# Attention backward: a PSUM bank of their own for the narrow gradient sums, and a two-step pattern of who turns dS

## The chip, the cores and the metric

The kernel runs on one core of a Trainium2 chip. The metric is the device time of one execution in microseconds (us), the median of several. A profile comes from one execution more, recorded with the hardware profiler: its span runs from the first to the last instruction.

## What is computed

Four layers are run forward and then differentiated: linear attention (A), sliding-window attention (B), A, B, each with a layer norm ahead and a residual around. The tensors are bfloat16, with 2,048 tokens, width 640, 32 heads of 20. The change lies in the backward of the two B layers. Their forward is:

```
scores = einsum("bhqd,bhkd->bhqk", q, k) * (Dh ** -0.5)
mask   = (idx[:, None] - idx[None, :] >= 0) & (idx[:, None] - idx[None, :] < 256)
p      = softmax(where(mask, scores, -1e9))
o      = einsum("bhqk,bhkd->bhqd", p, v)
out    = x + o.reshape(B, S, D) @ wo
```

The outputs are the result and the gradients of the input and of the four weight matrices.

## The kernel before

The program is the forward (L311 on), the backward's first phase, `B_attn_bwd` for layer 3 (L1291), a phase of projections and layer A, `B_attn_bwd` for layer 1, and a last phase. Only `B_attn_bwd` and its table `ORDER` (L37) are touched by the diff.

`B_attn_bwd` goes over 8 groups of 4 heads. A group has 16 tiles of 128 tokens and 15 steps, one for each query tile (the first step takes tiles 0 and 1 together): 120 steps. With a window of 256, a query tile sees three key tiles, so a step has three 128x128 blocks for each of 4 heads. Each step is cut into two half-steps of two heads, numbered h = 2n + p for step n, p 0 or 1. A half-step consists of

- `mm_s` (L1331, on TensorE): scores of two heads, into a `pair` tile in PSUM (128 x 2 x 512 float32, 4,096 bytes of a partition; three of them take turns);
- `act_exp` (L1351, ScalarE): the exponential, read from the pair tile, written to `e_sb`; GpSimd masks two of the three blocks (L1355, L1358);
- `mm_dp` (L1331): dP of the same two heads, into the same pair tile, over the scores;
- `dve_ds` (L1366, VectorE): dS = dP * e * scale, read from the pair tile and `e_sb`, written to `ds_sb`;
- the turn of dS, since dQ needs dS with the other axis ahead. Either TensorE turns it (`pe_turn`, L1384: six 128x128 transposes into a PSUM tile `dsT_ps`, 1,536 bytes of a partition, two of them) and VectorE or ScalarE copies it to SBUF (`copy_t`, L1387, into `dsT`), or a DMA turns it straight from `ds_sb` to `dsT` (`dma_turn`, issued by SyncE at L305);
- the narrow products (`products`, L1399 and L1403, TensorE): dQ, dK and dV of one token tile, 20 columns wide (padded to 32), summed over up to three blocks. Two heads take 18 matmuls of 128x32.

Where the narrow sums go: columns 384 to 480 of each half of a pair tile are free. `pair_acc` (L1410) writes the sums of two heads there, into the pair tile of half-step h + 2, and `pair_evac` (L1420) copies them out of it to `dqkv` (120 elements of a partition), by ScalarE or VectorE as the table says. In one step of each group but the first, two token tiles are ready; then `quad_acc` (L1423) puts all four heads of one of them into a `dsT_ps` buffer, and ScalarE copies 240 elements out of it (L1427).

The order of the work is written out by hand. Each piece gets a time in half-steps (L1464 to 1479) and the pieces are emitted in order of these times; each engine runs its own pieces in that order, and waits by semaphore for others. dS of half-step h stands at h, `mm_s` of h + 3 at h + 0.1, `mm_dp` of h + 2 at h + 0.15, `act_exp` of h + 3 at h + 0.7. The rest comes from `ORDER[p][kind]`: when to turn, when and on which engine to copy, when to do the narrow sums, when and on which engine to copy these. The kind is 0 for a step whose two halves are both turned by TensorE, 1 for a step whose second half is turned by DMA, 2 for such a step before another of its kind. `by_dma` (L1370) decides: within a group, steps 0, 2, 4 and 6 are turned by TensorE alone and the other eleven have their second half turned by DMA, except in the last six steps of all.

Between two engines that read the same pair tile the program puts a wait too: `dve_ds` of a half-step waits for the copy that takes narrow sums out of its pair tile.

Of the kernel before, what the change touches and what calls it, by code (L numbers as in the profile page):

```python
# [32 lines left out]
def dve_ns(n):  # L33
# [1 line left out]


ORDER = (  # L37
    ((0.3, 1.05, "ACT", 0.6, 1.6, "DVE"), (1.3, 2.25, "DVE", 0.6, 1.6, "ACT"), (2.3, 3.5, "DVE", 0.6, 1.05, "ACT")),
    ((0.7, 2.25, "DVE", 0.6, 1.3, "ACT"), (0.3, 1.8, "ACT", 0.6, 1.3, "ACT"), (2.05, 1.8, "DVE", 0.25, 1.3, "ACT")),
)  # L40


# [137 lines left out]
class Kern:  # L180
# [1110 lines left out]
    def B_attn_bwd(self, l, dqkv, slab0=None, first=None):  # L1291
        nc, tc, D, T, TT, H, G, DP = self.nc, self.tc, self.D, self.T, self.TT, self.H, self.G, self.DP
        ld, E, DS, PR, TPS, TSB, ACC = {}, {}, {}, {}, {}, {}, {}
        with ExitStack() as st:
            def pool(name, **kw):
                return st.enter_context(tc.tile_pool(name=f"Bb{l}_{name}", bufs=1, reuse_waits="tile", **kw))
# [3 lines left out]
            slab1, pe, pps = pool("slabB"), pool("pe"), pool("ps", space=bass.MemoryType.PSUM)  # L1300
# [9 lines left out]
            NB = TT - 1  # L1310
            NS = G * NB
# [28 lines left out]
            def mm_dp(h):  # L1340
                if h < 2 * NS:
                    by_head(h, PR[h], "dOT", "VT")
# [25 lines left out]
                    in1=E[n][:, hs], op0=ALU.mult, op1=ALU.mult)  # L1368

            def by_dma(n):  # L1370
                return n % NB not in (0, 2, 4, 6) and n < NS - 6

            def dma_turn(h):
                n, p = divmod(h, 2)
# [3 lines left out]

            def pe_turn(h):
                n, p = divmod(h, 2)  # L1380
                ps = TPS[h] = pps.tile([P, 2, 3, P], BF, name="dsT_ps", bufs=2)
                for i in range(2):
                    for j in range(3):
                        nc.tensor.transpose(ps[:, i, j, :], DS[n][:, 2 * p + i, j, :], self.ident)  # L1384

            def copy(eng, out, in_):
                (nc.vector.tensor_copy if eng == "DVE" else nc.scalar.copy)(out, in_)  # L1387
# [5 lines left out]
            def products(g, t, hhs, out):  # L1393
                dq = [(k, *place(g, t, k)) for k in range(max(t - 2, 0), t + 1)]
                dkv = [(q, *place(g, q, t)) for q in range(t, min(t + 3, TT))]
                for hh in hhs:
                    cs = slice(HPAD * hh, HPAD * (hh + 1))
                    for i, (k, n, j) in enumerate(dq):
                        nc.tensor.matmul(out(hh, 0), lhsT=TSB[2 * n + hh // 2][:, hh % 2, j, :],  # L1399
                                         rhs=ld[g]["K"][:, k, cs], start=(i == 0), stop=(i == len(dq) - 1))  # L1400
                    for x, (src, rhs) in enumerate(((DS, "Q"), (E, "dO"))):
                        for i, (q, n, j) in enumerate(dkv):
                            nc.tensor.matmul(out(hh, 1 + x), lhsT=src[n][:, hh, j, :],  # L1403
                                             rhs=ld[g][rhs][:, q, cs], start=(i == 0), stop=(i == len(dkv) - 1))

            def spare(h):

                return PR[h][:, :, 3 * P:3 * P + 3 * HPAD].rearrange("p i (s c) -> p i s c", c=HPAD)

            def pair_acc(g, t, p, h):  # L1410
                if h not in PR:
                    PR[h] = pps.tile([P, 2, 512], F32, name=f"pair{h % 3}")
                products(g, t, (2 * p, 2 * p + 1), lambda hh, x: spare(h)[:, hh % 2, x, :])

            def grads(g, t, hh, nh):
                o = (4 * g + hh) * DH
                return dqkv[:, t, :].rearrange("p (s x) -> p s x", s=3)[:, :, o:o + nh * DH].rearrange(
                    "p s (h d) -> p h s d", d=DH)

            def pair_evac(g, t, p, h, eng):  # L1420
                copy(eng, grads(g, t, 2 * p, 2), spare(h)[:, :, :, 0:DH])

            def quad_acc(g, t):  # L1423
                ACC[g, t] = pps.tile([P, 4, 3, HPAD], F32, name="dsT_ps", bufs=2)
                products(g, t, range(4), lambda hh, x: ACC[g, t][:, hh, x, :])

            def quad_evac(g, t, eng):  # L1427
                copy(eng, grads(g, t, 0, 4), ACC.pop((g, t))[:, :, :, 0:DH])

            outs = {}  # L1430
            for g in range(G):
# [7 lines left out]
            with tc.manual_schedule(engines={mybir.EngineType.PE, mybir.EngineType.DVE, mybir.EngineType.SP,  # L1439
                                             mybir.EngineType.Activation, mybir.EngineType.Pool}):  # L1440
                for h in range(3):
                    mm_s(h)
                    act_exp(h)
                for h in range(2):
                    mm_dp(h)
                items, todo = [], []

                def at(when, f, *args):
                    items.append((when, len(items), f, args))

                def load(n):
                    if n % NB == 0:
                        todo[:] = loads(n // NB + 1) if n // NB + 1 < G else next_weights()
                    if todo:
                        todo.pop(0)()

                for h in range(2 * (NS + 4)):
                    n, p = divmod(h, 2)
                    kind = 0 if not by_dma(n) else 2 if by_dma(n + 1) else 1
                    turn, cp, cp_eng, acc, ev, ev_eng = ORDER[p][kind]  # L1460
                    if n < NS:
                        if not p and n % NB % 2 == 0:
# [93 lines left out]
```

## Time and profile before

| | |
|---|---|
| median of 3 runs | 2328.52 us (2324.72 to 2328.61) |
| the profiled execution | 2327.18 us |
| its span | 2325.2 us |
| mean granted TensorE clock | 0.945 of full |
| TensorE, matmuls | 2023.2 us busy, 87% of the span |
| TensorE, weight loads | 1405.2 us, 60% |
| VectorE | 1463.7 us, 63% |
| ScalarE | 1182.6 us, 51% |
| GpSimd | 852.3 us, 37% |

PE is TensorE, PEld its weight loads, DVE VectorE, ACT ScalarE, POOL GpSimd, SP SyncE (SPq its queue). A row of the timeline reads: start in the span, length, engine, line of the kernel, operation, output <- input, shape, count, and in brackets the idle time of the engine just before and what ended it. In a row of waits stand the waiter, what ended the wait, the us in total, the number of times and the longest. A row by stretches gives the ends, the length, the busy us of PE, PEld, DVE, ACT and POOL with their instruction counts, the granted TensorE clock, the busy share of the DMA engines and GB/s. In a row by lines stand busy us and mean ns of one, then the idle time before. Matmuls overlap in TensorE's pipeline, so a busy PE is not a PE at its peak, and the distance from start to start tells more than the length.

Costly groups of the two stages, over the whole span:

```profile
L1366 DVE SCALAR_TENSOR_TENSOR ds_sb<-pair,e_sb 128x768 bf16<-128x768 f32 x480 | 457.5, 954 | 79.9 <-ACT dqkv L1387 43.9
L1351 ACT ACTIVATE e_sb<-pair 128x768 bf16<-128x768 f32 x480 | 389.6, 813 | 144.8 <-PE pair L1331 134.3
L1384 PE MATMUL dsT_ps<-ident,ds_sb 128*128 128x128 bf16 x1896 | 171.3, 231 | 0.5 <-ACT dsT L1387 0.3
```

### The profile page before, as it was taken

How to read it: one execution, taken by the hardware profiler on the slowest of the kernel's cores; microseconds unless marked ns; L12 is line 12 of the kernel's file. 1: busy time of each engine (PE TensorE's matmuls, PEld its weight loads, DVE VectorE, ACT ScalarE, POOL GpSimd, SP SyncE). 2: the span in 40 equal slices, each digit the busy share in tenths (PEclk: the TensorE clock that was granted, in tenths of full speed). 3: DMA queues.
4: the chain of work that ended last, by engine and by line, in shares of the span. 5: the costliest groups of instructions: out<-in, count | busy, mean ns of one | idle time of the engine just before them, and what ended most of it. 6: DMA issues, size and time to landing. Idle time of an engine off the chain costs nothing. (4 is left out here: it accounts for less than half of the span.)

```text
span 2325.2 us, 67576 instructions
## 1 busy us (share of the span) xinstructions
PE 2023.2 (87%) x27798; PEld 1405.2 (60%) x27798; DVE 1463.7 (63%) x3048; ACT 1182.6 (51%) x2091; POOL 852.3 (37%) x1851
## 2 busy tenths in 40 slices
PE   6879899888887688888889979997888888998999
PEld 4556566555555456666656657754666665665674
DVE  6657677555564488898943328912998885443551
ACT  4527787527787137787832213311888783210330
POOL 1015455315666245555522203311555552221120
PEclk9989999879999798899999989998999899998999
DMA  7658999646675768898887789737898988987973
GB/s 256 198 140 192 209 203 216 169 125 161 151 157 126 197 165 150 136 155 147 155 192 171 160 191 196 181 85 157 147 151 148 148 147 171 193 187 177 214 171 100
DMA packets 968103, 389.22 MB, mean 167 GB/s; under 512 B 860401, under 2 KB 939889, under 8 KB 967537
## 3 DMA queue, kind: packets, MB, share of 16 engines
q1 hardware_dynamic: 931488, 351.24, 72.7%
q10 hardware_dynamic: 36304, 33.67, 4.5%
q8 instruction: 217, 3.56, 0.7%
q14 instruction: 94, 0.76, 0.1%
HBM read 115.34 MB, written 114.95 MB: 99 GB/s over the span
## 5 line engine op out<-in xcount | busy, mean ns | idle before, releaser
L1366 DVE SCALAR_TENSOR_TENSOR ds_sb<-pair,e_sb 128x768 bf16<-128x768 f32 x480 | 457.5, 954 | 79.9 <-ACT dqkv L1387 43.9
L1351 ACT ACTIVATE e_sb<-pair 128x768 bf16<-128x768 f32 x480 | 389.6, 813 | 144.8 <-PE pair L1331 134.3
L626 ACT ACTIVATE e_sb<-s_ps 128x1536 bf16<-128x1536 f32 (+2 forms) x256 | 350.8, 1370 | 91.9 <-PE s_ps L621 44.6
L630 POOL TENSOR_SCALAR_AFFINE_SELECT e_sb<-e_sb 128x256 bf16<-128x256 bf16 x512 | 216.9, 447 | 457.2 <-ACT e_sb L626 455.0
L849 PEld LDWEIGHTS <-om 128*128 128x128 bf16 x1920 | 191.3, 100 | 179.9 <-DMA om<-o 21.5
L849 PE MATMUL mm_ps<-wq,dqT 128*128 128x320 bf16 x1920 | 282.3, 302 | 10.4 <-DMA dqT<-dqkv 10.2
L1358 POOL TENSOR_SCALAR_AFFINE_SELECT e_sb<-e_sb 128x256 bf16<-128x256 bf16 x448 | 183.0, 408 | 259.0 <-ACT e_sb L1351 253.7
L849 PE MATMUL mm_ps<-dqkv,om 128*128 128x480 bf16 x1280 | 271.2, 370 | 0.0
L1015 POOL TENSOR_TENSOR gw<-w,gcar 128x640 f32<-128x640 f32 x64 | 89.6, 1399 | 457.2 <-ACT w L1012 442.9
L1331 PE MATMUL pair<-KTg,QTg 32*128 32x384 bf16 (+2 forms) x1024 | 169.6, 336 | 93.3 <-DVE ds_sb L1366 80.0
L1355 POOL TENSOR_SCALAR_AFFINE_SELECT e_sb<-e_sb 128x256 bf16<-128x256 bf16 x512 | 207.4, 408 | 86.1 <-ACT e_sb L1351 86.1
L849 PEld LDWEIGHTS <-dqT 128*128 128x128 bf16 x1920 | 186.1, 99 | 84.9 <-DMA dqT<-dqkv 11.0
L1399 PE MATMUL pair<-Ksl,dsT 128*128 128x32 bf16 x2712 | 217.7, 179 | 0.0
L1403 PE MATMUL pair<-Qsl,ds_sb 128*128 128x32 bf16 x2824 | 214.0, 177 | 0.0
L1403 PE MATMUL pair<-dOsl,e_sb 128*128 128x32 bf16 x2824 | 213.8, 177 | 0.0
L997 ACT ACTIVATE dh<-mm_ps 128x320 f32<-128x320 f32 x128 | 56.0, 438 | 304.4 <-PE mm_ps L849 238.1
L399 PE MATMUL mm_ps<-Wqkv_B,hnTB 128*128 128x320 bf16 x960 | 184.2, 308 | 5.4 <-DMA hnTB<-hnB 3.8
L655 PEld LDWEIGHTS <-e_sb 128*128 128x128 bf16 x2880 | 130.7, 97 | 81.2 <-DVE e_sb L635 18.5
L1399 PEld LDWEIGHTS <-dsT 128*128 128x128 bf16 x2880 | 153.2, 98 | 42.6 <-issue 42.6
L1331 PE MATMUL pair<-VTg,dOTg 32*128 32x384 bf16 (+2 forms) x1024 | 169.7, 337 | 10.0 <-DMA dOTg<-dOpt 7.0
L655 PE MATMUL pv_ps<-v_slab,e_sb 128*128 128x32 bf16 x2880 | 155.3, 178 | 22.0 <-POOL e_sb L638 6.6
L1384 PE MATMUL dsT_ps<-ident,ds_sb 128*128 128x128 bf16 x1896 | 171.3, 231 | 0.5 <-ACT dsT L1387 0.3
(154 smaller groups left out, 3705.3 us busy)
## 6 DMA issues: line engine op xcount, KB each, us to landing
qkvp<-qk_slab SPq DMA_DIRECT2D x32, 512.0 KB, 3.1
e<-ee SPq DMA_DIRECT2D x32, 320.0 KB, 2.5
kv<-kv SPq DMA_DIRECT2D x32, 320.0 KB, 2.7
o<-o SPq DMA_DIRECT2D x64, 160.0 KB, 3.2
om<-o SPq DMA_DIRECT2D x20, 512.0 KB, 4.7
hn<-hn SPq DMA_DIRECT2D x64, 160.0 KB, 2.9
om<-hn SPq DMA_DIRECT2D x20, 512.0 KB, 4.7
ee<-e SPq DMA_DIRECT2D x32, 320.0 KB, 3.6
```

Source lines behind the costliest of these rows:

```text
L399: nc.tensor.matmul(ps.t[:, w0:w0 + width], lhsT=lhsT(), rhs=rhs(), start=start, stop=stop)
L626: op("ACT", av(4 * nkt * P), lambda: nc.scalar.activation(e.t[:, :, 0:nkt, :], s.t[:, :, 0:nkt * P].rearrange("p h (i q) -> p h i q", q=P) ...
L630: op("POOL", 440, lambda p_=p_: nc.gpsimd.affine_select(out=e.t[:, 2 * p_:2 * p_ + 2, nkt - 1, :], in_=e.t[:, 2 * p_:2 * p_ + 2, nkt - 1, ...
L655: nc.tensor.matmul(pv.t[:, h % 16, :], lhsT=e.t[:, hh, j, :], rhs=vts[j].t[:, h, :], start=(j == 0), stop=(j == nkt - 1))
L849: nc.tensor.matmul(ps.t[:, w0:w0 + width], lhsT=lhsT(), rhs=rhs(), start=start, stop=stop)
L1331: nc.tensor.matmul(ps[:, i, c0:c0 + len(ks) * P], lhsT=ld[g][lhs][r, q * P:(q + 1) * P], rhs=ld[g][rhs][r, ks[0] * P:(ks[-1] + 1) * P], st ...
L1351: nc.scalar.activation(e, PR[h][:, :, 0:3 * P].rearrange("p i (j q) -> p i j q", q=P), ACT.Exp, scale=self.c_att)
L1355: nc.gpsimd.affine_select(out=e[:, :, j, :], in_=e[:, :, j, :], compare_op=ALU.is_ge, fill=0.0, base=0, pattern=[[0, 2], [-1, P]], channel ...
L1358: nc.gpsimd.affine_select(out=e[:, :, j, :], in_=e[:, :, j, :], compare_op=ALU.is_ge, fill=0.0, base=-1, pattern=[[0, 2], [1, P]], channel ...
L1366: nc.vector.scalar_tensor_tensor(out=DS[n][:, hs], in0=PR[h][:, :, 0:3 * P].rearrange("p i (j q) -> p i j q", q=P), scalar=self.c_att, in1 ...
L1399: nc.tensor.matmul(out(hh, 0), lhsT=TSB[2 * n + hh // 2][:, hh % 2, j, :], rhs=ld[g]["K"][:, k, cs], start=(i == 0), stop=(i == len(dq) - 1))
L1403: nc.tensor.matmul(out(hh, 1 + x), lhsT=src[n][:, hh, j, :], rhs=ld[g][rhs][:, q, cs], start=(i == 0), stop=(i == len(dkv) - 1))
```

## The change

- Narrow sums get a PSUM tile of their own, `dqvk_ps` (1,536 bytes of a partition, one buffer), for all four heads of a token tile. `acc` writes two heads of it in each half-step, and `evac` copies all four out at once, always on ScalarE (240 elements of a partition). `pair_acc`, `pair_evac`, `quad_acc` and `quad_evac` go. Where a step has two token tiles, each half-step does all four heads of one.
- `dsT_ps` gets one buffer instead of two, which makes room for `dqvk_ps`.
- The kinds of steps now alternate in a group: even steps are turned by TensorE, both halves, and VectorE makes both copies; odd steps have their first half turned by TensorE and copied by ScalarE, and their second half turned by DMA. The last six steps of all have no DMA turn, as before.
- The times of the hand order are new: the first turn of an even step stands right behind its dS, `act_exp` at h + 0.4, the copies by VectorE at h + 1.8, which is before the dS of h + 2 on VectorE, `evac` at h + 1.3.

In numbers, for both stages: turns by TensorE 316 before, 374 after; turns by DMA 164 and 106; copies of a turned block by VectorE 240 and 268, by ScalarE 76 and 106; copies of narrow sums by VectorE 80 and 0, by ScalarE 404 of 120 elements with 14 of 240 before, 256 of 240 after. dS, exp, scores, dP and narrow matmuls stay the same in number.

On TensorE, the order of an even step A and an odd step B becomes: turn A0, scores and dP, narrow A0, turn A1, scores and dP, narrow A1, scores and dP, turn B0, narrow B0, scores and dP, narrow B1. On VectorE: dS A0, dS A1, copy A0, dS B0, copy A1, dS B1. On ScalarE: narrow copy of the step before, exp, exp, narrow copy of A, exp, copy B0, exp.

```diff
 ORDER = (
-    ((0.3, 1.05, "ACT", 0.6, 1.6, "DVE"), (1.3, 2.25, "DVE", 0.6, 1.6, "ACT"), (2.3, 3.5, "DVE", 0.6, 1.05, "ACT")),
-    ((0.7, 2.25, "DVE", 0.6, 1.3, "ACT"), (0.3, 1.8, "ACT", 0.6, 1.3, "ACT"), (2.05, 1.8, "DVE", 0.25, 1.3, "ACT")),
+    ((0.05, 1.8, "DVE", 1.05), (1.05, 1.06, "ACT", 1.05)),
+    ((0.05, 1.8, "DVE", 1.05), (None, None, None, 0.6)),
 )
...
             def by_dma(n):
-                return n % NB not in (0, 2, 4, 6) and n < NS - 6
+                return n % NB % 2 == 1 and n < NS - 6
...
-                ps = TPS[h] = pps.tile([P, 2, 3, P], BF, name="dsT_ps", bufs=2)
+                ps = TPS[h] = pps.tile([P, 2, 3, P], BF, name="dsT_ps")
...
-            def pair_acc(g, t, p, h):
-                if h not in PR:
-                    PR[h] = pps.tile([P, 2, 512], F32, name=f"pair{h % 3}")
-                products(g, t, (2 * p, 2 * p + 1), lambda hh, x: spare(h)[:, hh % 2, x, :])
...
-            def pair_evac(g, t, p, h, eng):
-                copy(eng, grads(g, t, 2 * p, 2), spare(h)[:, :, :, 0:DH])
...
+            def acc(g, t, hhs):
+                if (g, t) not in ACC:
+                    ACC[g, t] = pps.tile([P, 3, 4, HPAD], F32, name="dqvk_ps")
+                products(g, t, hhs, lambda hh, x: ACC[g, t][:, x, hh, :])
+
+            def evac(g, t):
+                o = 4 * g * DH
+                copy("ACT", dqkv[:, t, :].rearrange("p (s x) -> p s x", s=3)[:, :, o:o + 4 * DH].rearrange(
+                    "p s (h d) -> p s h d", d=DH), ACC.pop((g, t))[:, :, :, 0:DH])
...
-                    kind = 0 if not by_dma(n) else 2 if by_dma(n + 1) else 1
-                    turn, cp, cp_eng, acc, ev, ev_eng = ORDER[p][kind]
+                    turn, cp, cp_eng, narrow = ORDER[p][by_dma(n)]
...
-                        at(h + 0.7, act_exp, h + 3)
+                        at(h + 0.4, act_exp, h + 3)
...
-                            at(h + max(turn, cp) + 0.01, copy_t, h, cp_eng)
+                            at(h + cp, copy_t, h, cp_eng)
                     units = outs.get(n, [])
-                    if len(units) == 2 and not p:
-                        at(h + acc + 0.01, quad_acc, *units[0])
-                        at(h + acc + 0.62, quad_evac, *units[0], "ACT")
-                    for g, t in units[-1:]:
-                        at(h + acc, pair_acc, g, t, p, h + 2)
-                        at(h + ev, pair_evac, g, t, p, h + 2, ev_eng)
+                    heads = (0, 1) if p == 0 else (2, 3)
+                    if len(units) == 2:
+                        units, heads = [units[p]], range(4)
+                    for o in units:
+                        at(h + narrow, acc, *o, heads)
+                        if heads[-1] == 3:
+                            at(h + 1.3, evac, *o)
```

More of the change, by code (lines that the diff above doesn't have):

```diff
@@ L1404, in products @@
                                              rhs=ld[g][rhs][:, q, cs], start=(i == 0), stop=(i == len(dkv) - 1))
-            def spare(h):
-                return PR[h][:, :, 3 * P:3 * P + 3 * HPAD].rearrange("p i (s c) -> p i s c", c=HPAD)
-            def pair_acc(g, t, p, h):
-                if h not in PR:
-                    PR[h] = pps.tile([P, 2, 512], F32, name=f"pair{h % 3}")
-                products(g, t, (2 * p, 2 * p + 1), lambda hh, x: spare(h)[:, hh % 2, x, :])
[L1415 to L1418, printed above, removed]
-            def pair_evac(g, t, p, h, eng):
-                copy(eng, grads(g, t, 2 * p, 2), spare(h)[:, :, :, 0:DH])
[L1423 to L1428, printed above, removed]
+            def acc(g, t, hhs):
[6 more added lines that the diff above has]
+                    "p s (h d) -> p s h d", d=DH), ACC.pop((g, t))[:, :, :, 0:DH])
             outs = {}
```

## The prediction

> **What bounds the kernel now.** I read the busy time by stretches first. Two stretches hold the attention backward, one for each layer; the diff touches nothing else.
>
> ```profile
> 849.00:1176.00 327.00, 284.11 (x6284) 224.84 (x6282) 288.36 (x402) 257.41 (x486) 183.99 (x480) 0.92 0.85 149
> 1618.00:1941.00 323.00, 277.69 (x6285) 221.59 (x6286) 287.18 (x401) 256.21 (x484) 182.05 (x474) 0.96 0.89 149
> ```
>
> That is 327 and 323 us of the 2325.2 us span. No engine fills them: VectorE is busy 288 and 287 us, ScalarE 257 and 256. So something is waited for, and the view of waits (waiter, what ended the wait, us in total, times, longest) says what, here for the first stretch:
>
> ```profile
> ACT e_sb L1351 <- PE pair L1331: 50.4, 133, 1.1
> PE pair L1331 <- DVE ds_sb L1366: 38.9, 103, 0.8
> DVE ds_sb L1366 <- ACT dqkv L1387: 23.5, 68, 0.8
> ```
>
> The three engines wait for each other in a ring. The odd member is the last: VectorE's dS (L1366) waits for ScalarE to copy narrow sums into dqkv (L1387), whose values dS doesn't use. Both read the same pair tile in PSUM, and the program makes the second reader wait for the first. The timeline shows the ring closing (start, length, engine, line). A half-step is two heads of one query tile; dS runs once in each.
>
> ```profile
> 1117.77 1.95 DVE L1366 SCALAR_TENSOR_TENSOR ds_sb<-pair,e_sb 128x768 bf16<-128x768 f32 x2
> ...
> 1118.78 0.34 PE L1331 MATMUL pair<-KTg,QTg 32*128 32x384 bf16 x2 [0.50 <-DVE ds_sb L1366]
> 1119.06 0.51 PE L1384 MATMUL dsT_ps<-ident,ds_sb 128*128 128x128 bf16 x6
> 1119.16 0.81 ACT L1351 ACTIVATE e_sb<-pair 128x768 bf16<-128x768 f32 x1 [0.50 <-PE pair L1331]
> 1119.41 0.23 PE L1399 MATMUL pair<-Ksl,dsT 128*128 128x32 bf16 x3
> 1119.63 0.55 DVE L1387 COPY dsT<-dsT_ps 128x768 bf16<-128x768 bf16 x1
> 1119.94 0.34 PE L1331 MATMUL pair<-KTg,QTg 32*128 32x384 bf16 x2
> 1120.05 0.26 ACT L1387 CAST dqkv<-pair 128x120 bf16<-128x120 f32 x1
> 1120.32 0.81 ACT L1351 ACTIVATE e_sb<-pair 128x768 bf16<-128x768 f32 x1
> 1120.39 1.95 DVE L1366 SCALAR_TENSOR_TENSOR ds_sb<-pair,e_sb 128x768 bf16<-128x768 f32 x2 [0.21 <-issue]
> ```
>
> Follow one round: dS starts at 1117.77 and ends at 1118.73; TensorE, which waited for it, starts the next scores at 1118.78, turns dS at 1119.06 (six transposes), does the narrow products (L1399, L1403) from 1119.41; ScalarE takes them out at 1120.05 to 1120.31; only then, at 1120.39, the dS after next starts. A step (two half-steps) takes 2.62 us, although VectorE needs only 0.99 + 0.87 + 0.46 = 2.32 for it: dS to dS 0.99 (1.95 less 0.96), dS to copy 0.87 (1118.76 to 1119.63), copy to dS 0.46 by the rows below. These are "DMA steps", in which a DMA turns the second dS. A step in which TensorE turns both is a "PE step". Where the kinds alternate, two steps take 869.52 - 864.34 = 5.18 us, and the same wait stands there:
>
> ```profile
> 864.34 0.96 DVE L1366 SCALAR_TENSOR_TENSOR ds_sb<-pair,e_sb 128x768 bf16<-128x768 f32 x1 [0.43 <-ACT dqkv L1387]
> ...
> 868.75 0.49 PE L1384 MATMUL dsT_ps<-ident,ds_sb 128*128 128x128 bf16 x6
> 869.18 0.34 PE L1331 MATMUL pair<-KTg,QTg 32*128 32x384 bf16 x2
> ...
> 869.52 0.96 DVE L1366 SCALAR_TENSOR_TENSOR ds_sb<-pair,e_sb 128x768 bf16<-128x768 f32 x1 [0.43 <-ACT dqkv L1387]
> 869.55 0.81 ACT L1351 ACTIVATE e_sb<-pair 128x768 bf16<-128x768 f32 x1
> ...
> 870.40 0.55 DVE L1387 COPY dsT<-dsT_ps 128x768 bf16<-128x768 bf16 x1
> 870.43 0.41 POOL L1358 TENSOR_SCALAR_AFFINE_SELECT e_sb<-e_sb 128x256 bf16<-128x256 bf16 x1 [0.33 <-ACT e_sb L1351]
> 870.79 0.41 POOL L1355 TENSOR_SCALAR_AFFINE_SELECT e_sb<-e_sb 128x256 bf16<-128x256 bf16 x1
> 870.86 0.95 DVE L1366 SCALAR_TENSOR_TENSOR ds_sb<-pair,e_sb 128x768 bf16<-128x768 f32 x1
> ```
>
> Some steps are slower, because the granted clock falls:
>
> ```profile
> 885.48 0.96 DVE L1366 SCALAR_TENSOR_TENSOR ds_sb<-pair,e_sb 128x768 bf16<-128x768 f32 x1 [0.27 <-ACT dqkv L1387]
> ...
> 886.93 0.82 PE L1384 MATMUL dsT_ps<-ident,ds_sb 128*128 128x128 bf16 x6
> 887.54 0.29 PE L1399 MATMUL pair<-Ksl,dsT 128*128 128x32 bf16 x3
> 888.16 0.29 PE L1331 MATMUL pair<-KTg,QTg 32*128 32x128 bf16 x2
> ...
> 888.62 0.96 DVE L1366 SCALAR_TENSOR_TENSOR ds_sb<-pair,e_sb 128x768 bf16<-128x768 f32 x1 [0.27 <-ACT dqkv L1387]
> ```
> ```profile
> 880.00:890.00 10.00, 8.70 (x160) 6.36 (x159) 7.82 (x11) 6.35 (x14) 5.03 (x14) 0.50 0.97 146
> ...
> 900.00:910.00 10.00, 8.93 (x202) 7.00 (x199) 8.79 (x13) 8.45 (x17) 5.88 (x16) 1.00 0.70 146
> ...
> 1090.00:1100.00 10.00, 9.21 (x194) 7.11 (x190) 8.35 (x12) 7.22 (x14) 5.29 (x14) 0.72 0.52 102
> ```
>
> At clock 0.50 a DMA step takes 3.14 us (885.48 to 888.62). From the first dS to the last, the two stages take
>
> ```profile
> 849.54 0.96 DVE L1366 SCALAR_TENSOR_TENSOR ds_sb<-pair,e_sb 128x768 bf16<-128x768 f32 x1 [2.97 <-POOL e_sb L1355]
> ...
> 1170.43 1.95 DVE L1366 SCALAR_TENSOR_TENSOR ds_sb<-pair,e_sb 128x768 bf16<-128x768 f32 x2
> ...
> 1618.96 1.82 DVE L1366 SCALAR_TENSOR_TENSOR ds_sb<-pair,e_sb 128x768 bf16<-128x768 f32 x2 [13.61 <-PE pair L1331]
> ...
> 1935.25 1.96 DVE L1366 SCALAR_TENSOR_TENSOR ds_sb<-pair,e_sb 128x768 bf16<-128x768 f32 x2
> ```
>
> The last two rows with x2 hold two dS, 0.99 apart: 1171.42 - 849.54 = 321.9 and 1936.24 - 1618.96 = 317.3 us for 239 half-steps each, or 641.8 for all 480. A head group has 15 steps: eight alternating (4 x 5.18, and 0.3, worked out below, for the one step with two units of narrow sums) and seven DMA steps (7 x 2.62): 39.4 us, 630 for 16 groups. The other 12 us are cold steps.
>
> **The change, part by part.**
>
> *Narrow sums in a bank of their own.* dS no longer shares a tile with them, so its wait for ScalarE goes. What is late next follows from the new order of instructions. DMA steps and PE steps now alternate: 8 PE and 7 DMA steps in a group, so 7 pairs, and one more PE step where 14 meets 0. The turned dS has one PSUM buffer instead of two, so TensorE, which works in order, waits before the second turn of a PE step until VectorE has copied the first. Behind that turn stand the scores of a later half-step, their exp, and the next pair's first dS. This chain of a pair, from dS to the dS four half-steps on:
>
> - dS to the second dS 0.99; to the copy of the first turn 0.87;
> - the copy 0.55, and 0.05 until TensorE starts (1118.73 to 1118.78): 0.60;
> - the second turn to the scores behind it 0.43 (868.75 to 869.18);
> - scores to exp 0.38 (1119.94 to 1120.32);
> - exp to the masks on GpSimd 0.88 (869.55 to 870.43), second mask 0.36 later, its length 0.41, hand-off 0.05 as above: 1.70.
>
> Sum: 4.97 us a pair, against 5.18 alternating and 5.24 for two DMA steps. The extra PE step has two dS and two copies on VectorE: 2 x (0.87 + 0.46) = 2.66. With 0.3 for the step with two units (ten more narrow matmuls in a half, each 0.03: 18 from 1119.41 to 1119.94), a group takes 7 x 4.97 + 2.66 + 0.3 = 37.75 us; 16 groups take 604.
>
> *Can the engines carry it?* A pair has four dS and two copies on VectorE: 2 x 0.99 + 2 x 0.87 + 2 x 0.46 = 4.64. TensorE has three turns, four scores with dP, four narrow halves: at most 2 x 0.43 + 0.35 (1119.06 to 1119.41) + 4 x 0.35 + 4 x 0.53 (1119.41 to 1119.94) = 4.73, where 0.35 for scores with dP is on the high side (1118.78 to 1119.06 is 0.28). ScalarE has four exp, one copy of a turn and two narrow copies of 240 elements a partition, a shape that already occurs:
>
> ```profile
> 900.24 0.38 ACT L1387 CAST dqkv<-dsT_ps 128x240 bf16<-128x240 f32 x1
> ```
> ```profile
> L1387 ACT COPY dsT<-dsT_ps 128x768 bf16<-128x768 bf16 x38 | 30.1, 793 | 0.7 <-PE dsT_ps L1384 0.7
> ```
>
> In this order 4 x 0.81 + 0.79 + 2 x 0.38 = 4.79. All fit under 4.97, none by much.
>
> *What is added.* 29 more turns a stage on TensorE and 29 more copies (14 VectorE, 15 ScalarE), counted above. ScalarE loses some 200 narrow copies of 0.26 a stage and VectorE 40, and gets 128 of 0.38. *DMA:* 29 fewer transposes a stage leave the SyncE queue; in the view of waits nothing waits for one, so I count nothing, bounded by 0 and a fraction of a us. The earlier exp (0.4 instead of 0.7 in the hand order) is in the chain. *The end of a stage:* before, several pair tiles took turns and the next phase's matmuls start right behind the last narrow copy:
>
> ```profile
> 1940.60 0.26 ACT L1387 CAST dqkv<-pair 128x120 bf16<-128x120 f32 x1 [0.25 <-PE pair L1403]
> ...
> 1940.68 4.24 PE L849 MATMUL mm_ps<-wq,dqT 128*128 128x320 bf16 x30
> ```
>
> With one bank, each of the last four units waits for the copy of the one before: first narrow matmul to copy 0.64 (1119.41 to 1120.05), copy and hand-off 0.43, less the 0.53 that the narrow half takes anyway: 0.54 a unit, 2 us a stage, 4 in all (bounds 0 and 5).
>
> *Cold steps.* The alternating stretch is never cold here (1.00 in 900 to 910); the clock falls in runs of DMA steps (0.50 and 0.72 above). The new order has no such runs. I let 1.5 us of the 12 remain, for the start of the first stage.
>
> *Sum* against the profiled execution, 2327.2 us (span 2325.2): 641.8 - 604 = 37.8 less, 4 and 1.5 more: 2294.9. The median of the runs shown is 1.3 higher, 2328.5; so 2296, 32.5 us less.
>
> **The rivals.**
>
> *The clock (slower).* The granted clock falls to 0.50 in parts of the stages now; if the new order makes that common, the gain goes. A cold step of the new order takes at least (3 x 0.61 + 4 x 0.62 + 4 x 0.35)/2 = 2.86 us on TensorE (turns 886.93 to 887.54, narrow halves 887.54 to 888.16, scores as when warm), and 3.14 by the nearest row, the cold DMA step: 0.37 to 0.65 more than 4.97/2; I take 0.6. Cold in half of the 240 steps it adds 72: 2368. It decides from 32.5/0.6 = 54 cold steps on, about a quarter; before, 12 us at 0.52 (3.14 less 2.62) are 23. For it: TensorE gets more turns, which stream nothing but an identity. Against: the alternating stretch, with three turns in two steps, is the warm one, and the runs with two turns in two steps are the cold ones. 0.11. The Trainium skill, "TensorE: Matmul & The Clock Gate", Part 4, says that transposes on TensorE don't count as busy for the clock gate in the way matmuls do, which would make this rival the forecast. The trace so far disagrees: 1.00 from 900 to 910, 0.50 from 880 to 890.
>
> *A new wait takes the old one's place.* Narrow sums have one bank, so TensorE waits before the next unit until ScalarE has emptied it, and ScalarE does so only behind an exp. From the scores ahead of the last narrow half: exp after 0.38, 0.81 long, copy 0.38, hand-off 0.05: 1.62. TensorE comes back to the bank after 0.35 + 0.53 + 0.43 + 0.35 = 1.66. There is no room: each 0.1 that ScalarE is late costs 0.1 x 112 pairs = 11 us, and 0.29 eats the whole gain. With 0.3: 2296 + 33 = 2329. For it: that slack. Against: in the rows ScalarE's narrow copy starts 0.08 after its exp ends (1119.97 to 1120.05), so nothing else holds it. 0.10.
>
> *It doesn't do what it says.* dS still waits for the narrow copy through the order of ScalarE's queue, which holds both the copies and the exp that dS needs: the ring stays at 2.62 a step, 2328. Against: the exp that dS needs stands ahead of that copy in the queue. 0.04.
>
> *VectorE alone is the bound.* If TensorE's wait for the copy is hidden, a pair takes 4.64: 37 less, 2259. It needs the 0.88 from exp to mask to shrink, which no row shows. 0.06.
>
> **How the numbers follow.** Forecast 0.69, with its own range 2281 to 2314: hand-offs of 0.08 (1120.31 to 1120.39) in place of 0.05 at three or four joints of the chain move a pair by 0.1, 11 us; if all 12 cold us stay, 10.5 more. Faster by over 0.2% (4.7 us, about what a measurement of this kernel can tell from no change): 0.69 + 0.06 + 0.04 of the new wait = 0.79. Within: 0.04 + 0.03 = 0.07. Slower: 0.11 + 0.03 = 0.14. The range 2278 to 2328 leaves out the cold case, the VectorE case and the worst of the new wait, some 0.2.
>
> **What would show it.** Right: in the waits no line of dS on dqkv; dS four half-steps apart at 4.9 to 5.1 us; the stretches about 308 and 305 us; granted clock near 1.00 all through. The second turn of a PE step would start 0.05 after VectorE's copy ends. Wrong: narrow matmuls (L1399) that start right after ScalarE's copy of 128x240, a clock of 0.50 for more than a quarter of the stages, or dS that again starts 0.08 after a narrow copy ends.

## The result, and the profile after

The changed kernel takes 2299.76 us (median of 4 runs, 2296.44 to 2308.61) against 2326.8 us of the kernel before beside it (4 runs, 2324.72 to 2328.61): a ratio of 0.9885, with a 95% interval of 0.986 to 0.9909. That is 27 us less; 32.5 less were forecast. The profiled execution took 2298.88 us, its span is 2297.2 us, its mean granted clock 0.955.

First the stretches of the two stages, each from about 3 us ahead of the first dS to 2 us behind the last (columns as before):

```profile
849.00:1156.00 307.00, 296.79 (x6364) 217.82 (x6364) 285.05 (x375) 254.93 (x417) 183.42 (x480) 0.97 0.77 141
1601.00:1909.00 308.00, 296.10 (x6372) 218.05 (x6373) 285.39 (x374) 252.86 (x415) 181.26 (x474) 0.97 0.75 139
```

VectorE and ScalarE have about the work they had (285 and 255 us), in stretches 20 and 15 us shorter. TensorE is now busy for 97 and 96% of them. From the first dS to the last:

```profile
852.27 1.82 DVE L1366 SCALAR_TENSOR_TENSOR ds_sb<-pair,e_sb 128x768 bf16<-128x768 f32 x2 [2.96 <-POOL e_sb L1355]
...
1154.01 0.94 DVE L1366 SCALAR_TENSOR_TENSOR ds_sb<-pair,e_sb 128x768 bf16<-128x768 f32 x1
...
1604.49 1.82 DVE L1366 SCALAR_TENSOR_TENSOR ds_sb<-pair,e_sb 128x768 bf16<-128x768 f32 x2 [12.96 <-PE pair L1331]
...
1906.51 0.95 DVE L1366 SCALAR_TENSOR_TENSOR ds_sb<-pair,e_sb 128x768 bf16<-128x768 f32 x1
```

That is 301.7 and 302.0 us, where it was 321.9 and 317.3: 35.5 us less in sum. The waits, in and around the first stage (850 to 1160; waiter, what ended the wait, us, times, longest):

```profile
ACT e_sb L1351 <- PE pair L1331: 43.8, 81, 1.8
...
DVE ds_sb L1366 <- POOL e_sb L1355: 12.0, 38, 3.0
...
PE pair L1331 <- ACT e_sb L1351: 4.2, 10, 2.2
...
PE dqvk_ps L1399 <- ACT dqkv L1387: 1.3, 3, 0.5
```

The row of dS behind `dqkv` is gone. dS waits for the mask instead (12.0 us in 38 waits), and the one bank of narrow sums costs TensorE 1.3 us in three waits. The timeline of one pair shows the new chain, from dS to the dS four half-steps on:

```profile
1029.58 1.92 DVE L1366 SCALAR_TENSOR_TENSOR ds_sb<-pair,e_sb 128x768 bf16<-128x768 f32 x2 [0.20 <-POOL e_sb L1355]
...
1030.58 0.23 PE L1403 MATMUL dqvk_ps<-dOsl,e_sb 128*128 128x32 bf16 x3
...
1030.66 0.49 PE L1384 MATMUL dsT_ps<-ident,ds_sb 128*128 128x128 bf16 x6
...
1031.03 0.37 ACT L1387 CAST dqkv<-dqvk_ps 128x240 bf16<-128x240 f32 x1
...
1031.42 0.55 DVE L1387 COPY dsT<-dsT_ps 128x768 bf16<-128x768 bf16 x1
...
1031.86 0.23 PE L1403 MATMUL dqvk_ps<-dOsl,e_sb 128*128 128x32 bf16 x3
...
1032.02 0.49 PE L1384 MATMUL dsT_ps<-ident,ds_sb 128*128 128x128 bf16 x6
...
1032.45 0.34 PE L1331 MATMUL pair<-KTg,QTg 32*128 32x384 bf16 x2
...
1032.82 0.81 ACT L1351 ACTIVATE e_sb<-pair 128x768 bf16<-128x768 f32 x1 [0.55 <-PE pair L1331]
...
1034.06 0.41 POOL L1355 TENSOR_SCALAR_AFFINE_SELECT e_sb<-e_sb 128x256 bf16<-128x256 bf16 x1
...
1034.50 1.92 DVE L1366 SCALAR_TENSOR_TENSOR ds_sb<-pair,e_sb 128x768 bf16<-128x768 f32 x2 [0.20 <-POOL e_sb L1355]
```

dS to copy 1.84; the copy ends at 1031.97 and the second turn starts 0.05 later, 0.60 from the copy's start; turn to scores 0.43; scores to exp 0.37; exp to dS 1.68. The sum is 4.92 us. TensorE hardly waits in it: the second turn (1032.02) starts 0.16 after the start of the narrow matmuls in the row ahead of it, where the first turn (1030.66) starts 0.08 after those ahead of it. So the wait for the copy is worth some 0.08 us, and TensorE is nearly full beside this chain.

By the dS in the trace, a whole group of 15 steps takes 37.4 us. The first group of each stage takes 39.7 and 39.5, the last 38.6 and 39.2 (with 1.33 for the half-step behind the last dS). The first is cold, as the stretches say:

```profile
860.00:870.00 10.00, 9.97 (x169) 6.64 (x165) 7.91 (x11) 7.08 (x12) 5.10 (x14) 0.57 0.72 125
870.00:880.00 10.00, 9.84 (x223) 7.33 (x218) 9.48 (x13) 8.77 (x15) 6.27 (x17) 1.00 0.78 147
```

At the end of a stage, TensorE (first and third row) waits for the one bank, which ScalarE (second row) is emptying:

```profile
1909.36 0.23 PE L1399 MATMUL dqvk_ps<-Ksl,dsT 128*128 128x32 bf16 x3 [0.45 <-ACT dqkv L1387]
...
1910.45 0.36 ACT L1387 CAST dqkv<-dqvk_ps 128x240 bf16<-128x240 f32 x1 [1.14 <-PE dqvk_ps L1403]
...
1910.86 0.23 PE L1399 MATMUL dqvk_ps<-Ksl,dsT 128*128 128x32 bf16 x3 [0.45 <-ACT dqkv L1387]
...
1912.86 0.36 ACT L1387 CAST dqkv<-dqvk_ps 128x240 bf16<-128x240 f32 x1 [0.75 <-PE dqvk_ps L1403]
```

From the start of the last dS to the end of the last narrow copy it is 1913.22 - 1906.51 = 6.7 us here and 6.8 in the first stage; before it was 4.6 here and 4.3 in the first stage.

### The profile page after: what moved, and what is told of

It is laid out like the page before. It is cut to its first block, busy times and chain, and to the rows that moved or that the text cites. A ratio compares the mean times of both kernels' runs of the same rounds, so it can differ in the third digit from the quotient of the medians.

```text
span 2297.2 us, 68234 instructions
## 1 busy us (share of the span) xinstructions
PE 2057.8 (90%) x28146; PEld 1399.1 (61%) x28146; DVE 1461.4 (64%) x2996; ACT 1178.7 (51%) x1959; POOL 848.1 (37%) x1851
## 5 line engine op out<-in xcount | busy, mean ns | idle before, releaser
L1358 POOL TENSOR_SCALAR_AFFINE_SELECT e_sb<-e_sb 128x256 bf16<-128x256 bf16 x448 | 182.1, 406 | 229.1 <-ACT e_sb L1351 229.1
L1399 PE MATMUL dqvk_ps<-Ksl,dsT 128*128 128x32 bf16 x2880 | 225.8, 179 | 2.7 <-ACT dqkv L1387 2.7
L1403 PE MATMUL dqvk_ps<-dOsl,e_sb 128*128 128x32 bf16 x2880 | 220.4, 177 | 0.6 <-issue 0.6
L1403 PE MATMUL dqvk_ps<-Qsl,ds_sb 128*128 128x32 bf16 x2880 | 220.3, 177 | 0.0
L1384 PE MATMUL dsT_ps<-ident,ds_sb 128*128 128x128 bf16 x2244 | 191.9, 223 | 6.7 <-DVE dsT L1387 1.8
L1399 PEld LDWEIGHTS <-dsT 128*128 128x128 bf16 x2880 | 146.2, 96 | 67.1 <-issue 67.0
L1331 PE MATMUL pair<-VTg,dOTg 32*128 32x384 bf16 (+2 forms) x1024 | 164.7, 326 | 18.5 <-DMA dOTg<-dOpt 6.5
L1331 PE MATMUL pair<-KTg,QTg 32*128 32x384 bf16 (+2 forms) x1024 | 163.3, 328 | 6.8 <-DMA KTg<-qkvp 5.5
```

The source lines that it names most:

```text
L1331: nc.tensor.matmul(ps[:, i, c0:c0 + len(ks) * P], lhsT=ld[g][lhs][r, q * P:(q + 1) * P], rhs=ld[g][rhs][r, ks[0] * P:(ks[-1] + 1) * P], st ...
L1403: nc.tensor.matmul(out(hh, 1 + x), lhsT=src[n][:, hh, j, :], rhs=ld[g][rhs][:, q, cs], start=(i == 0), stop=(i == len(dkv) - 1))
```

## The experiments

The theory: the bank of its own takes dS's wait for ScalarE away, and the chain through the one turn buffer takes its place. The rivals: the gain comes from the alternation of the steps and the warmer clock with it; the bank has room to spare; another engine bounds the pair. Whatever has the bank below also has the new times of the hand order and the one turn buffer: no run separates these from the bank. Ratios are to the kernel before, with 95% intervals.

**1. The alternation alone.** The kernel before, with the new choice of steps; bank, copies and order stay as they were.

```diff
-                return n % NB not in (0, 2, 4, 6) and n < NS - 6
+                return n % NB % 2 == 1 and n < NS - 6
```

> The kernel before with one line changed: odd steps of a group have their second half turned by DMA, even steps by TensorE, as in the changed kernel; narrow sums stay in the pair tiles. Theory A (the gain comes from dS no longer waiting for the narrow copy): the ring stays, a pair takes 5.18 us, a group 7 x 5.18 + 2.6 + 0.3 = 39.2 us; only the cold steps of the runs of DMA steps go, at most 12 us: 2315 to 2325 us, and the waits still show dS on dqkv. Rival B (the gain comes from the alternation, which keeps TensorE's clock up and takes work from the DMA): nearly the whole gain, 2300 to 2306 us.

2316.85 us, ratio 0.995 (0.9929 to 0.997). Two rows by stretches and one of the waits:

```profile
880.00:890.00 10.00, 9.04 (x214) 7.30 (x211) 9.13 (x14) 8.43 (x16) 5.94 (x16) 1.00 0.70 146
...
1090.00:1100.00 10.00, 8.74 (x194) 6.79 (x191) 9.13 (x15) 8.39 (x17) 5.62 (x15) 1.00 0.66 90
```
```profile
DVE ds_sb L1366 <- ACT dqkv L1387: 24.5, 54, 0.8
```

Where the kernel before had 0.50 and 0.72, the clock is 1.00. The wait of dS for `dqkv` stays at 24.5 us (23.5 before, over a stretch of about the same length), and a pair takes 5.18 us, as it did. So the alternation saves most of the 12 us of cold steps (a warm group is also 0.2 us shorter, 39.2 for 39.4), and leaves the ring as it was.

**2. The bank alone.** The changed kernel, with the old choice of steps.

```diff
-                return n % NB % 2 == 1 and n < NS - 6
+                return n % NB not in (0, 2, 4, 6) and n < NS - 6
```

> The changed kernel with the old rule for which steps a DMA turns (eleven of fifteen). Theory A: no wait of dS on dqkv; the eight alternating steps stay at 4.92 us a pair, a DMA step falls from 2.62 to between VectorE's 2.32 and 2.45, a group to about 36.5 us, so 2283 to 2292 us if the clock stays at 1.00; with cold stretches as before the change (12 us of 16 groups) about 2300. Rival B (alternation is what helps): most of the gain is lost, 2315 us or more, with granted clock 0.5 in the runs of DMA steps.

2293.0 us, ratio 0.9848 (0.9825 to 0.9871), just above the range of theory A. It is a little faster than the whole change; the two intervals overlap, but from the first dS to the last the stages of its trace take 297.4 and 298.2 us, 8.2 less in sum. One group, from its first dS to that of the next, and a stretch in a run of DMA steps:

```profile
966.66 1.92 DVE L1366 SCALAR_TENSOR_TENSOR ds_sb<-pair,e_sb 128x768 bf16<-128x768 f32 x2 [0.51 <-PE dsT_ps L1384]
...
1003.54 1.92 DVE L1366 SCALAR_TENSOR_TENSOR ds_sb<-pair,e_sb 128x768 bf16<-128x768 f32 x2 [0.51 <-PE dsT_ps L1384]
```
```profile
1030.00:1040.00 10.00, 9.48 (x210) 6.78 (x209) 7.80 (x9) 10.00 (x18) 6.35 (x18) 1.00 1.33 162
```

The group takes 36.9 us. Runs of DMA steps are now warm (1.00), at 2.45 us a step, with ScalarE busy for the whole of the 10 us; the alternating pairs are at 2.43 + 2.49 as in the changed kernel. So the alternation isn't needed for the clock once the ring is gone. It costs 0.5 us a group, 8 in all. With it, step 14 and step 0 are both PE steps, and the second of them takes 2.67 instead of 2.43; the other half of the 0.5 lies in the steps behind it, and why is open.

**3. The second row's turn behind the scores.** Takes the scores, and so exp, out from behind the turn that waits for the copy.

```diff
-    ((0.05, 1.8, "DVE", 1.05), (None, None, None, 0.6)),
+    ((0.2, 1.8, "DVE", 1.05), (None, None, None, 0.6)),
```

> The changed kernel with one number changed: in an even step the second turn stands behind the scores and dP of its half-step (0.2) instead of ahead of them (0.05). Theory A' (the pair's 4.92 us are the chain over VectorE's copy of the first turn, the second turn, the scores, exp and masks): the wait for the copy no longer holds the scores, a pair falls to 4.8 to 4.87 us, 6 to 13 us in all: 2287 to 2294 us. Rival C (TensorE is simply full, busy 9.84 of 10 us, and its waits are only the gaps left over): within 3 us of the changed kernel, 2297 to 2303 us.

2299.85 us, ratio 0.988 (0.986 to 0.99): the time of the changed kernel. A pair, and one of the last steps:

```profile
1030.14 2.87 DVE L1366 SCALAR_TENSOR_TENSOR ds_sb<-pair,e_sb 128x768 bf16<-128x768 f32 x3
...
1034.98 2.87 DVE L1366 SCALAR_TENSOR_TENSOR ds_sb<-pair,e_sb 128x768 bf16<-128x768 f32 x3
```
```profile
1138.06 0.95 DVE L1366 SCALAR_TENSOR_TENSOR ds_sb<-pair,e_sb 128x768 bf16<-128x768 f32 x1
...
1141.15 0.95 DVE L1366 SCALAR_TENSOR_TENSOR ds_sb<-pair,e_sb 128x768 bf16<-128x768 f32 x1
```

The pair falls to 4.84, so the turn was in the chain, and it is worth 0.08, the wait of the second turn for the copy. TensorE is then busy for 9.8 to 10.0 of 10 us in the rows from 1030 to 1070, as here:

```profile
1050.00:1060.00 10.00, 10.00 (x220) 7.62 (x218) 9.70 (x13) 9.01 (x16) 6.12 (x16) 1.00 0.92 150
```

But the last six steps, all PE steps, take 3.09 each instead of 2.66, and step 0 of a group 2.85. The gain and the loss cancel.

**4. One mask.** The changed kernel without the mask of the oldest block (L1358), which it leaves out of the computation.

```diff
-                    elif k == t - 2:
-                        nc.gpsimd.affine_select(out=e[:, :, j, :], in_=e[:, :, j, :], compare_op=ALU.is_ge, fill=0.0,
-                                                base=-1, pattern=[[0, 2], [1, P]], channel_multiplier=-1)
```

> The changed kernel without the mask of the oldest block (line 1358 of the kernel), which is left out of the computation; GpSimd then has one mask behind each exp, and dS may start 0.36 us earlier after it. Theory A': that 0.36 is in the chain, so a pair falls from 4.92 towards the next bound, 4.64 (VectorE) to 4.75 (TensorE): 19 to 31 us less in 112 pairs, 2269 to 2281 us. Rival C (TensorE is full): no change within 4 us, 2296 to 2304 us.

2291.47 us, ratio 0.9844 (0.9826 to 0.9862), between the two expectations. The dS (here L1363) at 1031.70 now waits for dP of TensorE, not for a mask, and 4.83 us is the mean of a pair:

```profile
1031.70 0.96 DVE L1363 SCALAR_TENSOR_TENSOR ds_sb<-pair,e_sb 128x768 bf16<-128x768 f32 x1 [0.23 <-PE pair L1331]
```

So the masks are in the chain, but only 0.09 of the 0.36 that one of them takes comes back. The next bound stands at 4.83, right behind the chain; both shortened chains, this one and that of the third experiment, stop there.

**5. Narrow sums copied twice.** ScalarE copies the bank twice in a row, the same values to the same place.

```diff
-                copy("ACT", dqkv[:, t, :].rearrange("p (s x) -> p s x", s=3)[:, :, o:o + 4 * DH].rearrange(
-                    "p s (h d) -> p s h d", d=DH), ACC.pop((g, t))[:, :, :, 0:DH])
+                sums = ACC.pop((g, t))
+                for _ in range(2):
+                    copy("ACT", dqkv[:, t, :].rearrange("p (s x) -> p s x", s=3)[:, :, o:o + 4 * DH].rearrange(
+                        "p s (h d) -> p s h d", d=DH), sums[:, :, :, 0:DH])
```

> The changed kernel, with each narrow copy made twice in a row by ScalarE (the same values to the same place), so that the one bank comes free 0.37 us later, once a step. Theory A, the prediction's count of that bank: it has no room (ScalarE back after 1.62, TensorE at the bank after 1.66), so every delay shows in full, 0.3 to 0.37 a pair where one of its two units is tight: 34 to 42 us more, 2334 to 2342 us, and waits of the narrow products for the narrow copy appear in the steady steps. Rival: the bank has room, and ScalarE only fills up: its 8.77 of 10 us are 4.31 a pair of 4.92, with 2 x 0.37 more 5.05, so a pair takes 5.05 and the time is 15 us more, 2315 us, with ScalarE busy 10 of 10 and no such waits.

2366.34 us, ratio 1.0171 (1.0138 to 1.0204): slower than before the change. ScalarE's two copies (x2) and the narrow matmuls behind them, for the two steps of a pair:

```profile
1041.53 0.74 ACT L1387 CAST dqkv<-dqvk_ps 128x240 bf16<-128x240 f32 x2
...
1042.33 0.23 PE L1399 MATMUL dqvk_ps<-Ksl,dsT 128*128 128x32 bf16 x3
...
1044.25 0.78 ACT L1387 CAST dqkv<-dqvk_ps 128x240 bf16<-128x240 f32 x2
...
1045.09 0.23 PE L1399 MATMUL dqvk_ps<-Ksl,dsT 128*128 128x32 bf16 x3 [0.30 <-ACT dqkv L1387]
```

Both times TensorE starts 0.06 after the copies end: the bank is now the bound, 2.76 us a step instead of 2.46. A copy that is 0.37 longer costs 0.30, so the bank has some 0.07 us of room a step. That there is no room to speak of was right. The price was too low by half, and this is an error of the prediction's rival as well: it counted one late unit in a pair, and there are two, so each 0.1 beyond the room costs 0.1 x 240 = 24 us, not 11.

**6. Narrow sums taken out by VectorE.** One word: "ACT" becomes "DVE" in `evac`.

```diff
-                copy("ACT", dqkv[:, t, :].rearrange("p (s x) -> p s x", s=3)[:, :, o:o + 4 * DH].rearrange(
+                copy("DVE", dqkv[:, t, :].rearrange("p (s x) -> p s x", s=3)[:, :, o:o + 4 * DH].rearrange(
```

> The changed kernel, with the narrow sums taken out by VectorE at the same place of the hand order, nothing else. Theory A: who takes them out matters for where VectorE's queue is held, not for the sum of its work alone. The copy then stands on VectorE between a step's second dS and the next copy of a turned block, waits there for the narrow products, and the copy of the turn, on which TensorE waits, stands behind it: about 0.5 us a step more, 2400 to 2440 us. Rival, only VectorE's load counts: 9.49 of 10 us busy are 4.67 a pair, two narrow copies of about 0.35 make it 5.37, 0.45 a pair over 4.92, 50 us more: 2350 us.

2461.47 us, ratio 1.0578 (1.0543 to 1.0613). The waits from 850 to 1200:

```profile
DVE dqkv L1387 <- PE dqvk_ps L1403: 48.7, 78, 1.4
PE dsT_ps L1384 <- DVE dsT L1387: 46.1, 104, 1.0
```
```profile
849.00:1233.00 384.00, 323.29 (x6327) 229.04 (x6327) 320.26 (x496) 233.03 (x293) 183.36 (x480) 0.86 0.60 113
```

VectorE waits for the narrow products, and TensorE for the copy of a turned block behind that wait. VectorE is busy 320 of 384 us: it is held, not full. By the dS in the trace, a warm pair takes 3.14 + 2.74 = 5.88 us, 0.48 a step more than before this edit, as expected. So this is the queue and not the load. That the time lies above the expected 2400 to 2440 goes with the granted clock, which falls to 0.86 here; the expectation left that out.

**7. The end of a stage in pair tiles.** The last units of narrow sums go to pair tiles, which no scores use any more.

```diff
-                    ACC[g, t] = pps.tile([P, 3, 4, HPAD], F32, name="dqvk_ps")
+                    if g == G - 1 and t + 2 >= NB:
+                        ps = pps.tile([P, 2, 512], F32, name=f"pair{t % 3}")
+                        ACC[g, t] = ps[:, 0, :12 * HPAD].rearrange("p (s h c) -> p s h c", s=3, c=HPAD)
+                    else:
+                        ACC[g, t] = pps.tile([P, 3, 4, HPAD], F32, name="dqvk_ps")
```

> The changed kernel, with the narrow sums of the last three or four units of a stage put into pair tiles, which no scores use any more by then, instead of the one bank. Theory A: the one bank makes the end of a stage 2.2 us longer, since each unit waits for the copy of the one before; with other tiles the distance from the last dS to the end of the last narrow copy falls from 6.7 and 6.8 us to 4.5 to 5, and the time by about 4 us: 2296 us. Rival: the end is held by the turn and copy of the last dS, and the three waits of 0.45 that the trace shows are all there is to win, or nothing: the distance stays at 6 or more and the time is 2298 to 2300 us.

2294.15 us, ratio 0.9862 (0.9825 to 0.9899). The last dS and the last narrow copy of the second stage:

```profile
1903.20 0.95 DVE L1366 SCALAR_TENSOR_TENSOR ds_sb<-pair,e_sb 128x768 bf16<-128x768 f32 x1
```
```profile
1907.75 0.36 ACT L1387 CAST dqkv<-pair 128x240 bf16<-128x240 f32 x1 [0.15 <-PE pair L1403]
```

1908.11 - 1903.20 = 4.9 us in place of 6.7, and 4.9 in place of 6.8 in the first stage: 3.7 of the 4.5 us are won back, so the one bank made most of the longer end.

**8 to 10. Versions.** All three have the bank, the end of the seventh experiment, and DMA turns up to the last two steps instead of the last six. The eighth has the old choice of steps, and VectorE copies the first turn of every DMA step, where ScalarE was full in the second experiment:

```diff
-    ((0.05, 1.8, "DVE", 1.05), (1.05, 1.06, "ACT", 1.05)),
+    ((0.05, 1.8, "DVE", 1.05), (0.2, 1.8, "DVE", 1.05)),
...
-                return n % NB % 2 == 1 and n < NS - 6
+                return n % NB not in (0, 2, 4, 6) and n < NS - 2
```

> The bank alone, with the old choice of steps (0, 2, 4 and 6 of a group turned by TensorE, eleven with a DMA turn), and three edits to it: DMA turns up to the last two steps instead of the last six, the end of a stage in pair tiles, and the copy of the first turn in DMA steps by VectorE instead of ScalarE, which had 10 of 10 us busy in these runs. Theory A (ScalarE bounds runs of DMA steps at 2.45 us, and VectorE's 2.32 would be next): steps of 2.35 to 2.40 there, some 100 steps by 0.07, 7 us; with 2 us from the last steps and 3 from the end, 2293 less 12: 2281 us. Rival (ScalarE is full there only because it is given the work, and the step is held by the chain over TensorE): steps stay at 2.45 or rise to 2.49, 2288 to 2293 us.

2305.19 us, ratio 0.9907 (0.988 to 0.9933): worse than the bank alone. Runs of DMA steps did fall to 2.39 us. The alternating pairs rose to 5.29:

```profile
1020.51 0.95 DVE L1366 SCALAR_TENSOR_TENSOR ds_sb<-pair,e_sb 128x768 bf16<-128x768 f32 x1
...
1023.13 0.56 DVE L1387 COPY dsT<-dsT_ps 128x768 bf16<-128x768 bf16 x1 [0.34 <-PE dsT_ps L1384]
...
1025.80 0.95 DVE L1366 SCALAR_TENSOR_TENSOR ds_sb<-pair,e_sb 128x768 bf16<-128x768 f32 x1
```

There VectorE now waits 0.34 for a turn on TensorE, with the next dS behind it. The expectation didn't count the pairs. The ninth therefore keeps ScalarE for a DMA step that follows a PE step:

```diff
-    ((0.05, 1.8, "DVE", 1.05), (0.2, 1.8, "DVE", 1.05)),
-    ((0.05, 1.8, "DVE", 1.05), (None, None, None, 0.6)),
+    ((0.05, 1.8, "DVE", 1.05), (1.05, 1.06, "ACT", 1.05), (0.2, 1.8, "DVE", 1.05)),
+    ((0.05, 1.8, "DVE", 1.05), (None, None, None, 0.6), (None, None, None, 0.6)),
...
-                    turn, cp, cp_eng, narrow = ORDER[p][by_dma(n)]
+                    turn, cp, cp_eng, narrow = ORDER[p][by_dma(n) + (by_dma(n) and by_dma(n - 1))]
```

> The bank alone with the old choice of steps, the end of a stage in pair tiles, DMA turns up to the last two steps, and the copy of the first turn by VectorE only in a DMA step that follows a DMA step; a DMA step behind a PE step keeps ScalarE. Theory A, from the run that gave VectorE all of these copies (2.39 a step in runs of DMA steps, 5.28 a pair where the kinds alternate) and the run of the bank alone (2.45 and 4.92): the two simply combine, a group takes 36.9 less 7 x 0.06 = 36.5 us, with 2 us from the last steps and 4 from the ends of the stages 2293 less 13: 2280 us (2276 to 2285). Rival: the joints between the kinds cost what the run of steps gains, the group stays at 36.9 or more and only the ends are won: 2286 to 2290 us.

2288.19 us, ratio 0.9835 (0.9812 to 0.9857). Runs of DMA steps are at 2.39 and pairs at 4.92, but the first step of a run that VectorE copies for takes 2.91, and the group 37.0: the rival was right, and only the ends were won. Against the second experiment's 2293.0 the intervals overlap. The tenth turns the second half of every step up to the last two by DMA:

```diff
-                return n % NB not in (0, 2, 4, 6) and n < NS - 2
+                return n < NS - 2
```

> As the one before, but every step up to the last two is a DMA step, with VectorE's copy: 236 DMA turns in place of the changed kernel's 106, no pairs at all. Theory A, what bounds a DMA step is VectorE and the half-step's chain, not the DMA: 15 x 2.39 + 0.3 = 36.2 us a group, 5 us less than the mixed kernel: 2275 us (2270 to 2280). Rival, the DMA engines, at 0.97 to 1.09 of a busy share in the runs of DMA steps, can't carry the loads of the next group beside a turn in every step: narrow products wait for turned blocks, some steps go to 3 us, the clock falls, and the time is 2300 us or more.

2311.43 us, ratio 0.9931 (0.9911 to 0.995). A wait that no other kernel here shows, and the stretch behind one of them:

```profile
PE dqvk_ps L1399 <- DMA dsT<-ds_sb: 10.1, 12, 1.1
```
```profile
900.00:910.00 10.00, 9.25 (x169) 6.47 (x166) 6.98 (x10) 5.69 (x10) 4.71 (x13) 0.56 1.05 187
```

Narrow products wait for turned blocks, and cold steps of 3.0 us follow. The steps between are at 2.39. So with a DMA turn in every step the DMA comes late, and turns by TensorE in part of the steps avoid that.

## Why the prediction was right, and where it wasn't

*The ring.* Right: dS's wait for `dqkv` is gone, and it goes with the bank and not with the alternation (experiments 1 and 2). How much of the gain is the bank's, and how much is due to the new times of the hand order, such as the earlier exp, no run shows.

*The pair.* Forecast 4.97, measured 4.92, each joint within 0.02 of its row. Seven pairs in 16 groups make 112 x 0.05 = 5.6 us less than forecast. What stood next was further up than I had it: the engines' bounds were put at 4.64 to 4.79, and the chain, shortened twice, stopped at 4.83 and 4.84. In the third experiment the profile points to TensorE, busy for up to 10.00 of 10 us at 4.84 a pair; in the changed kernel 9.84 of 10 us at 4.92 are 4.84 too. I had put its work at 4.73 at most, so this term seems too small by 0.11, and the chain that I forecast binds by only 0.08. In the fourth, TensorE is busy for 9.6 to 9.9 of 10 us in the same rows, and what stops it at 4.83 is less clear. No run takes TensorE's work away alone, so this stays argued.

*Cold steps.* The count was wrong: 1.5 us forecast, 4.3 measured, since the first group of both stages has five cold steps (39.7 and 39.5 us against 37.4); I had put a cold start at the first stage only, by half of that. The size isn't fixed: in the seventh experiment, which does the same work there, three steps of each first group are cold (38.3 us both times). The reason was wrong too. I took the runs of DMA steps to be cold by their kind. The second experiment has the same runs without the ring, warm, and the first has the ring without the runs, warm from 865 to the last dS of its first stage. So in these two neither is enough by itself; which event sets off a cold spell in the kernel before stays open. The Trainium skill, "TensorE: Matmul & The Clock Gate", Part 4, says that transposes don't count as busy for the clock in the way that matmuls do. No run bears it out: the changed kernel, with the most turns on TensorE, is at 1.00 from 870 to the last dS of the first stage, and cold spells in many groups come in the tenth experiment, with the fewest turns there, and in the sixth, with as many as the changed kernel but long waits for their copies. No run isolates it either, since other matmuls stand between the turns everywhere. Part 1 of that page of the Trainium skill says that TensorE gets its full clock after at least one busy window of about 3.4 us; in the row from 860 to 870 it is busy for 9.97 of 10 us, and the mean clock is 0.57.

*The last six steps.* Not in the sum: all of them are PE steps, at 2.66 instead of 2.46 each (two in the second stage at 3.02 and 2.81), so the two last groups together took 2.9 us more than twice 37.4.

*The stages together.* 2 x 8 groups: 16 x 37.42 = 598.7, 4.3 at the start, 2.9 at the end and 0.4 in single steps make 606.3; forecast were 604 and 1.5. That the sum came so close is luck: the pair was 5.6 too long, and the cold steps and the last steps were 5.7 too short.

*The end of a stage.* 4 us forecast for both, 2.4 and 2.1 measured, 4.5 in sum. The seventh experiment shows that most of it is the one bank.

*The start.* The first dS came 2.7 us later (852.27, before 849.54), in code that the change doesn't touch; this was in no sum. In the nine kernels that have the bank and were run in the experiments it stands between 850.75 and 854.40, in the first experiment, without it, at 850.25. The stage's first scores are later by the same 2.7 us (847.27, before 844.55), so the delay arises ahead of the stage. Whether the change moves it or it varies by itself stays open.

*Sum.* On the span 35.5 less in the stages, 4.5 more at their ends, 2.7 at the start, 0.3 elsewhere: 28.0 less, where 32.3 less were forecast.

*The rivals.* The clock: the mean over the stages is 0.97, cold steps are ten and not 54. The new wait: it didn't come, by 0.07 us a step, and at 0.37 it made the kernel 1.7% slower, a price twice the one I gave. VectorE alone: the pair stands at 4.92, not 4.64. The change does what it says.

## What to carry to other kernels

- When two engines read one PSUM tile for different reasons, look in the waits for a row in which an engine waits for a value that it doesn't use. Here it held steps of 2.62 us in a ring with no engine full, and a tile of its own, with an order of the work to go with it, was worth 1.5%.
- Before you trust a gain from a single buffer, put a price on its room: double the copy that empties it. Here it had 0.07 us a step, and a longer copy, or one on another engine, turned 1.1% faster into 1.7% and 5.8% slower.
- Run the parts of a change alone. The alternation of steps helped by itself (0.5%) and cost some 0.3% beside the bank (8 us by the traces), which removes the same cold steps, makes runs of DMA steps as fast as pairs, and needs no PE step next to another.

## What the runs showed of the hardware

- TensorE's granted clock can stay at 0.50 for some 17 us (about 851.6 to 868.6) at the start of a stage, though in the last 8 of them TensorE has no gap to speak of in the trace; then it goes to 1.00 and stays there to the last dS, with turns and narrow matmuls mixed:

```profile
860.00:864.00 4.00, 4.00 (x59) 2.55 (x56) 3.27 (x5) 2.58 (x4) 2.34 (x7) 0.50 0.60 133
864.00:868.00 4.00, 4.00 (x74) 2.65 (x69) 3.24 (x5) 2.67 (x4) 1.86 (x6) 0.50 0.89 110
```

- The kernel before had 0.99 from 860 to 870 already, though TensorE was less busy there (9.28 of 10 us), and the seventh experiment was cold for some 10 us only (854 to 864). What wakes the clock, the runs don't show. In the first stage of the tenth experiment each of five cold spells, 7 to 24 us at 0.50, begins 0.3 to 2.7 us after the end of a wait of 0.6 to 1.1 us for a DMA; other such waits have none behind them.
- With a DMA turn in every step, 236 instead of 106 or 164, the DMA is late here and there: 12 waits in some 300 us of the first stage, up to 1.1 us each.
